# Five unread GpSimd multiplies behind every three indirect DMAs, pinned in program order

## The chip, the cores and the metric

The kernel runs on one core of one Trainium2 chip. The metric is the device time of one execution, in microseconds (us). The core's engines are named as the profile names them: PE (TensorE, the matrix multiplies; PEld its weight loads), DVE (VectorE), ACT (ScalarE), POOL (GpSimd) and SP (SyncE, which issues most of the DMAs). Each engine works through its own instructions in order; semaphores hold an instruction until what it needs is done.

## The reference

Attention in which a query sees only the keys of its own cluster, and behind it a feed-forward network (FFN) with three hidden products of which the largest is kept.

```python
batch, n_heads, seq, head_dim = (4, 8, 768, 64)      # 16 clusters per head
q_assign = argmax(q_n @ c_n)                          # nearest centroid of each query
k_assign = argmax(k_n @ c_n)                          # and of each key
mask = q_assign[:, :, :, None] == k_assign[:, :, None, :]
scores = where(mask, scale * q @ k.T, -1e9)
attn_out = softmax(scores) @ v
x = attn_out.transpose(0, 2, 1, 3).reshape(3072, 512)
h = maximum(maximum(x @ w1, x @ w2), x @ w3)          # 512 -> 768
out = h @ w_out                                       # 768 -> 512
```

## The kernel before, in words

The kernel doesn't compute all 768 x 768 scores. It sorts the tokens of each head by cluster into 1024 places (8 blocks of 128), so that only 8 blocks of 128 x 128 scores are needed. The sorting of keys and values, and the way back of the outputs, are done by indirect DMAs that POOL issues. A (batch, head) is called a head below; there are 32, in 4 batches of 8.

For each head, in this order:

- `split_kv` (L554 on ACT, L555 on DVE) scales keys and values and splits them into a high and a low half-precision part, `kv`.
- `scatter` (L578, POOL): 6 indirect DMAs, one for each tile of 128 tokens, write rows of `kv` to their places in a buffer in device memory. Four such buffers are used in turn (`ring`, `kv_0` to `kv_3`). A scatter has a bounds check, for which POOL's sequencer sets a register just ahead of each DMA.
- `read_back` (L602 and the lines after it, SP) brings the sorted keys and values back as `kt` and `vt`.
- `order_q` (L622 on DVE builds one-hot rows `hot`; L624 on PE) sorts the queries by matrix multiply.
- `scores` (PE, DVE L660, ACT L665, DVE L670) and `values` (L684 to L686 on PE, L689 on DVE) make the outputs `of` of the sorted places, which SP writes to one of four buffers in device memory (`o_0` to `o_3`).
- `gather` (L699, POOL): 6 indirect DMAs fetch the rows of the head back in token order into `xb`, one tile of 128 tokens each. `xb` holds a whole batch, and there is one of it.

When the 8 heads of a batch are gathered, `x_split` (L273 on ACT, L274 on DVE, transposed by SP at L730) prepares the FFN's input; the FFN runs as L741 (hidden layers, PE, with DVE L753 and L758) and L774 (output, PE, with ACT L783). The FFN of batches 0 to 2 is spread over the heads of the next batch. The FFN of batch 3 can only come at the end.

The order of the work is set by a priority that a plan gives to each unit; a scheduler then lists each engine's instructions by these priorities and by when it takes their inputs to be ready. For head `k` of 32, the plan puts `scatter` at `k - 2.5` and `gather` at `k + 1.6`:

```python
put(max(k + h - 2, 0), when(k + h - 2.5, k), u["scatter"][h])
put(min(k + 1 + LATE, B * H), when(k + 0.6 + LATE, k), gather, b, h)
```

At the start POOL builds small tables for about 25 us; among these is `side` (128 x 4), made at L142, which eight multiplies `s_x * side` at L150 read.

Of the kernel before, what the change touches and what calls it, by code (L numbers as in the profile page):

```python
# [8 lines left out]
F32 = mybir.dt.float32  # L9
# [6 lines left out]
ALU = mybir.AluOpType  # L16
# [7 lines left out]
def sorted_attn__then__maxout_ffn(  # L24
# [17 lines left out]
    nc = tc.nc  # L42
# [3 lines left out]
    P = 128  # L46
# [27 lines left out]

    def const(shape, dt, name):
        return cpool.tile(shape, dt, name=name)

    def after(x, o, why=mybir.DependencyReason.DATA):
        tc.add_manual_dep(
            x.ins, o.ins.name, mybir.DependencyInfo(mybir.DependencyClass.Sync, why), reason="one of several places"  # L80
        )


    ident = const([P, P], F32, "ident")
    make_identity(nc, ident)
    ident16 = const([P, P], BF16, "ident16")
    nc.gpsimd.tensor_copy(ident16, ident)
    identh = const([P, P], F16, "identh")
    nc.gpsimd.tensor_copy(identh, ident)
    cw = const([P, H, 2 * C], F32, "cw")  # L90
# [51 lines left out]
    side = const([P, 4], F32, "side")  # L142
# [356 lines left out]
    def pair_units(b, pr):  # L499
# [67 lines left out]
        def index(h, n, u):  # L567
            a = 2 * (2 * (pr & 1) + h) + u
            return fours[b, pr // 2]["idx"][:, n, a : a + 1]
# [3 lines left out]
        def scatter(h):  # L573
            def f():
                at = (2 * g + h) % NRING
                sent = d["sent", h] = []
                for n in range(QT):
                    i = nc.gpsimd.indirect_dma_start(  # L578
                        out=ring[at],
                        out_offset=bass.IndirectOffsetOnAxis(ap=index(h, n, 1), axis=0),  # L580
                        in_=d["kv", h][:, n].rearrange("p a d -> p (a d)"),
                        in_offset=None,
                        bounds_check=NPLACE - 1,
                        oob_is_err=False,
                    )
                    for o in sent:
                        tc.declare_no_dep(i.ins, o.ins, reason="each place is one token's")
                    for o in ring_last[at]:
                        after(i, o, mybir.DependencyReason.ANTI)
                    sent.append(i)  # L590
                ring_last[at] = []

            return f
# [99 lines left out]
    def gather(b, h):  # L693
        d, i = st[b, h // 2], h & 1
        od = oring[(b * H + h) % NOUT]
        if b not in xb:
            xb[b] = sb.tile([P, QT, DM], F32, tag="xb", name="xb", bufs=NXB)
        for n in range(QT):
            nc.gpsimd.indirect_dma_start(  # L699
                out=xb[b][:, n, h * D : h * D + D],  # L700
                out_offset=None,
                in_=od,
                in_offset=bass.IndirectOffsetOnAxis(ap=d["index"](i, n, 0), axis=0),
            )

    x16, xsc = {}, {}

# [125 lines left out]
    for b in range(B):  # L833
        for h in range(H):
            k = b * H + h
            put(k, when(k, k), scores, b, h)
            put(k + 1, when(k + 0.5, k), values, b, h)
            put(min(k + 1 + LATE, B * H), when(k + 0.6 + LATE, k), gather, b, h)
        k = b * H + H + LATE
        if b + 1 < B:  # L840
            put(k + 1, k - 0.5, x_scale, b)
            for n in range(QT):
                put(k + 1, k - 0.5 + 0.01 * n, x_split, b, n)
            units = [u for gi in range(NG) for u in ffn_units(b, gi)]
            spread(units, k + 1, k + H + 1 + (F2 if b == 2 else 0), 0)
# [778 lines left out]
```

## Time and profile before

| | |
|---|---|
| median of 3 runs | 772.13 us (768.11 to 774.67) |
| profiled execution | 773.91 us, of which 772.2 us are the span of the profile |
| mean granted clock of PE | 0.885 of full speed |
| busy share of the span | PE 80%, DVE 61%, POOL 55%, ACT 53% |
| POOL's indirect DMAs | 384: 192 scatters and 192 gathers |

A row of a group of instructions gives the line, engine and operation, the tiles written and read, how often it ran, its busy time and the mean duration of one in ns, and then how long the engine stood idle just ahead of these instructions and what ended that idle time. An idle time put down to "issue" is one in which the engine waited for nothing that the profile shows.

### The profile page before, as it was taken

How to read it: one execution, taken by the hardware profiler on the slowest of the kernel's cores; microseconds unless marked ns; L12 is line 12 of the kernel's file. 1: busy time of each engine (PE TensorE's matmuls, PEld its weight loads, DVE VectorE, ACT ScalarE, POOL GpSimd, SP SyncE). 2: the span in 40 equal slices, each digit the busy share in tenths (PEclk: the TensorE clock that was granted, in tenths of full speed). 3: DMA queues.
4: the chain of work that ended last, by engine and by line, in shares of the span. 5: the costliest groups of instructions: out<-in, count | busy, mean ns of one | idle time of the engine just before them, and what ended most of it. 6: DMA issues, size and time to landing. Idle time of an engine off the chain costs nothing.

```text
span 772.2 us, 12828 instructions
## 1 busy us (share of the span) xinstructions
PE 621.5 (80%) x4284; PEld 352.6 (46%) x4313; DVE 473.8 (61%) x1202; ACT 410.9 (53%) x978; POOL 426.4 (55%) x478
## 2 busy tenths in 40 slices
PE   3466446566527899999999998988799999999993
PEld 1233223334314465555455655644366465564651
DVE  4787867887588888586769765775554324121220
ACT  2567665977585666564867655565644413211111
POOL 6374577777765467777767575767276544000000
PEclk8579756557658899999999999999899999999998
DMA  9778879999699567898976656477845434200001
GB/s 319 272 214 188 224 179 221 271 220 255 180 265 184 138 144 204 172 217 172 215 172 162 130 135 176 118 154 138 163 90 113 120 77 84 69 1 28 14 1 46
DMA packets 231197, 120.54 MB, mean 156 GB/s; under 512 B 200656, under 2 KB 209872, under 8 KB 231120
## 3 DMA queue, kind: packets, MB, share of 16 engines
q1 hardware_dynamic: 218832, 100.72, 55.1%
q0 software_dynamic: 12288, 18.90, 9.7%
q8 instruction: 36, 0.59, 0.3%
q14 instruction: 41, 0.34, 0.1%
HBM read 58.75 MB, written 29.36 MB: 114 GB/s over the span
## 4 chain that ended last, share of the span: by engine, by line
PE 42%; DMA 15%; issue 13%; POOL 12%; DVE 9%; ACT 6%; SPq 2%; POOLq 0%; DVEq 0%; ACTq 0%
PE one L741 24%; PE one L774 9%; POOL kv L578 6%; POOL xb L699 5%; PE big L624 4%; DMA kv<-kv,cl_idx 4%; DMA xb<-o,cl_idx 3%; ACT e L665 2%; DMA o<-of 2%; DMA x<-xh 2%; DVE hot L622 2%; DMA wd<-in_moe_w_dram 1%; DVE kv L555 1%; DMA kt<-kv 1%; PE big L656 1%
## 5 line engine op out<-in xcount | busy, mean ns | idle before, releaser
L741 PE MATMUL one<-x,w 128*128 128x384 f16 x1728 | 296.6, 329 | 12.4 <-DVE wf_h L753 4.0
L699 POOL DMA_INDIRECT xb<-o,cl_idx x192 | 195.5, 1018 | 132.8 <-DMA o<-of 70.5
L578 POOL DMA_INDIRECT kv<-kv,cl_idx x192 | 212.5, 1107 | 85.0 <-issue 51.5
L741 PEld LDWEIGHTS <-w 128*128 128x128 f16 x1728 | 168.8, 99 | 126.7 <-issue 20.1
L624 PE MATMUL big<-hot,q 128*128 128x512 f16 x384 | 122.9, 442 | 47.9 <-DVE q L565 19.8
L665 ACT ACTIVATE e<-big,nm,sc_al 128x128 f32<-128x128 f32 x256 | 113.6, 462 | 29.2 <-DVE nm L661 16.2
L622 DVE TENSOR_SCALAR hot<-line,cl_code 128x1024 f16<-128x1024 f16 x192 | 92.3, 498 | 5.5 <-PE big L624 5.1
L624 PEld LDWEIGHTS <-q 128*128 128x128 f16 x384 | 37.6, 107 | 92.7 <-issue 46.9
L753 DVE SCALAR_TENSOR_TENSOR wf_h<-one,wf_h 128x384 f32<-128x384 f32 x48 | 26.6, 554 | 55.4 <-PE one L741 55.3
L753 DVE SCALAR_TENSOR_TENSOR vf_h<-one,vf_h 128x384 f32<-128x384 f32 x48 | 26.7, 555 | 51.0 <-PE one L741 51.0
L665 ACT ACTIVATION_READ_ACCUMULATOR e<-big,nm,sc_al 128x1 f32 x256 | 53.4, 209 | 0.0
L774 PE MATMUL one<-wo,wf_h 128*128 128x512 f16 x216 | 49.3, 386 | 1.5 <-ACT o L783 0.8
L774 PE MATMUL one<-wo,vf_h 128*128 128x512 f16 x216 | 48.7, 379 | 1.4 <-ACT o L783 1.4
L660 DVE TENSOR_REDUCE nm<-big 128x8 f32<-128x1024 f32 x32 | 39.0, 1217 | 16.0 <-PE big L658 8.6
L684 PE MATMUL one<-vt,pt 128*128 128x64 f16 x256 | 29.5, 203 | 21.3 <-DMA pt<-hl 18.9
L632 ACT CAST qt<-big 128x1024 f16<-128x1024 f32 x32 | 32.5, 1014 | 22.0 <-PE big L624 17.0
L783 ACT ACTIVATE o<-one,so 128x512 f32<-128x512 f32 x24 | 15.9, 685 | 51.4 <-PE one L774 40.0
L515 ACT ACTIVATE junk<-rows 128x768 bf16<-128x768 f32 x32 | 27.0, 843 | 30.1 <-DVE cl_code L467 20.0
L670 DVE SCALAR_TENSOR_TENSOR hl<-e,hl 128x1024 f16<-128x1024 f32 x32 | 38.9, 1214 | 5.4 <-ACT hl L669 5.3
L554 ACT ACTIVATE kv<-rows,sc_s 128x384 f16<-128x384 f32 x64 | 35.8, 613 | 8.7 <-DVE sc_s L542 8.7
L689 DVE TENSOR_TENSOR of<-one,r 128x512 f32<-128x512 f32 x32 | 21.9, 685 | 29.6 <-PE one L686 27.5
L555 DVE SCALAR_TENSOR_TENSOR kv<-rows,sc_s,kv 128x384 f16<-128x384 f32 x64 | 37.5, 611 | 2.8 <-ACT kv L554 2.7
(212 smaller groups left out, 890.3 us busy)
## 6 DMA issues: line engine op xcount, KB each, us to landing
stage<-in_qk_dram SPq DMA_DIRECT2D x32, 384.0 KB
wd<-in_moe_w_dram SPq DMA_DIRECT2D x18, 512.0 KB
vt<-kv SPq DMA_DIRECT2D x32, 256.0 KB
o<-of SPq DMA_DIRECT2D x32, 256.0 KB
rows<-in_kr_dram SPq DMA_DIRECT2D x16, 384.0 KB
rows<-in_v_dram SPq DMA_DIRECT2D x16, 384.0 KB
rows<-in_qr_dram SPq DMA_DIRECT2D x16, 384.0 KB
out_dram<-o SPq DMA_DIRECT2D x24, 256.0 KB
```

The costliest lines, as they stand in the source:

```text
L554: nc.scalar.activation(kv[:, :, at], x, AF.Copy, scale=s[:, i : i + 1])
L555: nc.vector.scalar_tensor_tensor(kv[:, :, at + 1], x, s[:, i : i + 1], kv[:, :, at], op0=ALU.mult, op1=ALU.subtract)
L578: i = nc.gpsimd.indirect_dma_start(out=ring[at], out_offset=bass.IndirectOffsetOnAxis(ap=index(h, n, 1), axis=0), in_=d["kv", h][:, n].rea ...
L622: nc.vector.tensor_scalar(a, line, code, None, op0=ALU.is_equal)
L624: nc.tensor.matmul(t[:, lo : lo + 512], d["q16"][:, h * QT + n].rearrange("p a d -> p (a d)"), a[:, lo : lo + 512], start=(n == 0), stop=( ...
L660: nc.vector.tensor_reduce(nm, ts, axis=AX.X, op=ALU.max)
L665: nc.scalar.activation(x[:, j], ts[:, j], AF.Exp, bias=nm[:, j : j + 1], scale=d["al"], accum_out=sm[:, j : j + 1])
L670: nc.vector.scalar_tensor_tensor(hl[:, 1], x, 2.0**14, hl[:, 0], op0=ALU.mult, op1=ALU.subtract)
L699: nc.gpsimd.indirect_dma_start(out=xb[b][:, n, h * D : h * D + D], out_offset=None, in_=od, in_offset=bass.IndirectOffsetOnAxis(ap=d["inde ...
L741: nc.tensor.matmul(t[:, 0:NB], w16[:, jt, wa, i, ct], x16[b, gi][:, :, xa * CT + ct, :], start=(n == 0), stop=(n == 3 * CT - 1),)
L753: nc.vector.scalar_tensor_tensor(m, t[:, 0:NB], 2.0**-23, ms[jt], op0=ALU.mult, op1=ALU.max)
L774: nc.tensor.matmul(t[:, 0:DM], h16[jt][:, ha, tt * P : (tt + 1) * P], wo16[:, jt, wa, :], start=(n == 0), stop=(n == 3 * JT - 1),)
```

## The change

A 128 x 4 tile `blank` is added. `scatter` and `gather` call a new function `spaced` behind each of their 6 indirect DMAs (n = 0 to 5). It pins the DMA, except for n = 0, behind the instruction that was written last on POOL, and behind n = 2 and n = 5 it adds five multiplies `blank = side * side` on POOL, each pinned in the same way. Nothing reads `blank`.

```diff
+    blank = const([P, 4], F32, "blank")
+
+    def spaced(i, n):
+
+        if n:
+            tc.keep_in_program_order(i)
+        for _ in range(5 if n % 3 == 2 else 0):
+            tc.keep_in_program_order(nc.gpsimd.tensor_tensor(blank, side, side, op=ALU.mult))
...
                     for o in ring_last[at]:
                         after(i, o, mybir.DependencyReason.ANTI)
+                    spaced(i, n)
                     sent.append(i)
...
-            nc.gpsimd.indirect_dma_start(
+            got = nc.gpsimd.indirect_dma_start(
                 out=xb[b][:, n, h * D : h * D + D],
...
+            spaced(got, n)
```

A pin is an order of issue on one engine and no wait. But all the multiplies write the same tile, so each one also waits on a semaphore until the one before it is done; they form one chain in the order in which they are written. In all there are 32 heads x 2 x 2 x 5 = 640 of them. The line of the scatter becomes L587, that of the gather L709, and the multiplies stand at L85.

On POOL, where the scatters and gathers begin, the order before was this (`kv16` is the head's `kv` tile, and a row that ends in x6 is six instructions in a row):

```order
L578 DMA kv_0_226<-kv16_394,cl_idx_352 1024x256 x6
L578 DMA kv_1_227<-kv16_414,cl_idx_352 1024x256 x6
L578 DMA kv_2_228<-kv16_459,cl_idx_352 1024x256 x6
L578 DMA kv_3_229<-kv16_544,cl_idx_352 1024x256 x6
L699 DMA xb_952<-o_0_231,cl_idx_352 128x64 x6
```

At the same place the changed kernel has this:

```order
L587 DMA kv_0_227<-kv16_395,cl_idx_353 1024x256 x3
L85 TENSOR_TENSOR blank_72<-side_119 128x4
L587 DMA kv_0_227<-kv16_395,cl_idx_353 1024x256 x3
L587 DMA kv_1_228<-kv16_415,cl_idx_353 1024x256 x6
L85 TENSOR_TENSOR blank_72<-side_119 128x4 x4
L587 DMA kv_2_229<-kv16_470,cl_idx_353 1024x256
L85 TENSOR_TENSOR blank_72<-side_119 128x4
L587 DMA kv_2_229<-kv16_470,cl_idx_353 1024x256 x5
L85 TENSOR_TENSOR blank_72<-side_119 128x4
L587 DMA kv_3_230<-kv16_565,cl_idx_353 1024x256 x6
L85 TENSOR_TENSOR blank_72<-side_119 128x4 x33
L709 DMA xb_1003<-o_0_232,cl_idx_353 128x64 x3
```

The scatters aren't parted by five multiplies: the instruction written last ahead of a scatter is the setting of its register, so its pin holds it behind that and not behind the multiplies, and these are put off and stand in bunches, here 33 ahead of the first gather. The gathers have no such register and are parted as written.

At the end of the heads, the last rows of POOL before were these gathers, of heads 26 to 31 if the first is 0:

```order
L699 DMA xb_6692<-o_2_233,cl_idx_5094 128x64 x6
L699 DMA xb_6692<-o_3_234,cl_idx_5094 128x64 x6
L699 DMA xb_6692<-o_0_231,cl_idx_6106 128x64 x6
L699 DMA xb_6692<-o_1_232,cl_idx_6106 128x64 x6
L699 DMA xb_6692<-o_2_233,cl_idx_6106 128x64 x6
L699 DMA xb_6692<-o_3_234,cl_idx_6106 128x64 x6
```

In the changed kernel the last twelve rows are these, halves of the gathers of heads 28 to 31:

```order
L709 DMA xb_7223<-o_0_232,cl_idx_6587 128x64 x3
L85 TENSOR_TENSOR blank_72<-side_119 128x4 x10
L709 DMA xb_7223<-o_1_233,cl_idx_6587 128x64 x3
L85 TENSOR_TENSOR blank_72<-side_119 128x4
L709 DMA xb_7223<-o_2_234,cl_idx_6587 128x64 x3
L85 TENSOR_TENSOR blank_72<-side_119 128x4 x9
L709 DMA xb_7223<-o_2_234,cl_idx_6587 128x64 x3
L85 TENSOR_TENSOR blank_72<-side_119 128x4
L709 DMA xb_7223<-o_3_235,cl_idx_6587 128x64 x3
L85 TENSOR_TENSOR blank_72<-side_119 128x4 x9
L709 DMA xb_7223<-o_3_235,cl_idx_6587 128x64 x3
L85 TENSOR_TENSOR blank_72<-side_119 128x4 x5
```

Each head's gather has become two halves with multiplies between and ahead of them. Over the whole program the 640 multiplies stand in 93 bunches, of 1 to 33. The scheduler has also moved instructions of the other engines against each other; from the last values on, PE and DVE have the same order as before.

## The prediction

> **What bounds the kernel now.** I read the rows of busy time by slice first, then the busy time by stage, then POOL's groups and waits, and the chain at the end.
>
> ```profile
> PE   3466446566527899999999998988799999999993
> POOL 6374577777765467777767575767276544000000
> ```
>
> PE is full only from about a third of the span on. POOL looks half busy throughout and has nothing to do in the last sixth. By stage, from the first scatter to the last gather and beyond:
>
> ```profile
> core 0: us, PE busy (x) PEld busy (x) DVE busy (x) ACT busy (x) POOL busy (x), PEclk, DMA share, GB/s
> 100.00:200.00 100.00, 60.18 (x408) 32.83 (x411) 78.52 (x207) 74.75 (x173) 77.97 (x72) 0.64 0.95 228
> 250.00:400.00 150.00, 142.41 (x1095) 83.14 (x1103) 117.54 (x312) 95.73 (x236) 102.04 (x98) 0.98 0.83 183
> 400.00:550.00 150.00, 133.97 (x972) 78.12 (x979) 100.63 (x236) 88.43 (x225) 99.54 (x93) 0.97 0.63 143
> 651.00:772.00 121.00, 107.88 (x608) 59.27 (x606) 24.88 (x45) 21.24 (x39) 0.00 (x0) 0.97 0.11 30
> ```
>
> From 100 to 200 us POOL's 72 DMAs take 78 us; from 250 to 550 us PE is busy for 276 of 300 us. But busy time understates POOL, as its own timeline shows (start, duration, and in brackets the idle time ahead):
>
> ```profile
> 113.02 1.09 POOL L699 DMA_INDIRECT xb<-o,cl_idx  x1 [0.30 <-issue]
> 114.41 0.94 POOL L699 DMA_INDIRECT xb<-o,cl_idx  x1 [0.30 <-issue]
> 115.66 1.14 POOL L699 DMA_INDIRECT xb<-o,cl_idx  x1 [0.30 <-issue]
> ```
>
> Between two indirect DMAs POOL loses 0.30 us in which nothing is waited for. So 72 of them fill 78 + 72 x 0.30 = 99.6 of the 100 us: in that stage POOL is full. The groups and their real waits for the whole run:
>
> ```profile
> L578 POOL DMA_INDIRECT kv<-kv,cl_idx x192 | 212.5, 1107 | 85.0 <-issue 51.5 <-DVE kv L555 28.0 <-DMA xb<-o,cl_idx 0.9
> L699 POOL DMA_INDIRECT xb<-o,cl_idx x192 | 195.5, 1018 | 132.8 <-DMA o<-of 70.5 <-issue 53.3 <-DVE xh L274 5.6
> POOL xb L699 <- DMA o<-of: 70.5, 14, 14.0
> POOL kv L578 <- DVE kv L555: 28.0, 5, 12.1
> POOL xb L699 <- DVE xh L274: 5.6, 1, 5.6
> POOL xb L699 <- DVE worow L322: 2.7, 1, 2.7
> ```
>
> The idle time adds up to 85.0 + 132.8 = 217.8 us. The four waits make 70.5 + 28.0 + 5.6 + 2.7 = 106.8; the other 111.0 are the 0.30 gaps. The tables ahead of the first scatter and the last gather have these rows:
>
> ```profile
> 22.27 2.79 POOL L170 TENSOR_SCALAR k_line<-k_line,block 128x128 f16<-128x128 f16 x8
> 649.51 1.30 POOL L699 DMA_INDIRECT xb<-o,cl_idx  x1 [0.30 <-issue]
> span 772.2 us, 12828 instructions
> ```
>
> So POOL's path is closed: 25.06 us of tables (22.27 + 2.79), 408.0 us in DMAs, 111.0 us in gaps and 106.8 us of waiting give 650.9 us, which is where the last gather ends (649.51 + 1.30 = 650.8). **POOL is bound for 544 of its first 651 us, and only 107 us of slack lie in them.** Behind that comes a tail in which POOL has no part:
>
> ```profile
> 653.93 11.81 PE one L774 x54
> 665.75 35.10 PE one L741 x216
> 713.49 35.10 PE one L741 x216
> ```
>
> From the end of the last gather to the end of the span it is 772.2 - 650.8 = 121.4 us: the FFN of batch 3, and ahead of it the L774 block of batch 2, whose last DVE step is queued behind the split of the last gathered tiles.
>
> **The change part by part.** It removes nothing. It adds 640 multiplies to POOL, and it moves DMAs.
>
> *One multiply.* The trace has eight of the same shape and operation, at L150:
>
> ```profile
> L150 POOL TENSOR_TENSOR s_x<-s_x,side 128x4 f32<-128x4 f32 x8 | 1.6, 198 | 0.3
> 17.26 0.20 POOL L150 TENSOR_TENSOR s_x<-s_x,side 128x4 f32<-128x4 f32 x1
> 17.39 0.13 POOL L149 MEMSET s_x<- 128x1 f32 x2
> 17.60 0.20 POOL L150 TENSOR_TENSOR s_x<-s_x,side 128x4 f32<-128x4 f32 x1
> ```
>
> It takes 0.198 us. The instruction behind one at 17.26 needs nothing of it and starts 0.13 us later, so an unchained multiply costs POOL 0.13 us. The multiply at 17.60 needs the memsets that end at 17.39 + 0.13 = 17.52 and starts 0.08 us behind them. A chained one, which waits for its predecessor's end, should cost 0.198 + 0.08 = 0.28 us. The `blank` multiplies are all chained, so I take 0.28: **640 x 0.28 = 179 us** more on POOL's path. Ends: 640 x 0.13 = 83 us if the chain doesn't keep them from overlapping; for the upper end see the third rival.
>
> *The gap of 0.30 us.* The trace doesn't show whether it stands ahead of an indirect DMA or behind it, since nothing else ever stands between two. If a bunch fills a gap, 93 bunches save up to 93 x 0.30 = 28 us; if a gap stands on both sides of a bunch, they cost 28 us more. I take none, which lies between.
>
> *What the 179 us meet.* The slack is 106.8 us. Two parts of it can be placed: the first wait, 10.75 of the 28.0 us on L555, stands ahead of the first scatter, with no multiply ahead of it, and stays. The longest, 14.0 us ahead of the first gather, has a bunch of 33 in front (33 x 0.28 = 9.2 us) and shrinks to 5. The other 82 us are some 18 waits for outputs (`o<-of`) or split keys, most of them after 220 us. As the DMAs slow down, each head has more time to become ready, so most of these go; a bunch that stands behind a wait doesn't hide in it, though, and in-order queues on SP and DVE can hold a head up for a late gather. I keep a quarter, 20 us, which makes 36 us of waiting left. Ends: none of the rest, 16; or all of it, 107.
>
> *What is queued behind the waits.* Behind each multiply that waits stand gathers and scatters. A late scatter holds SP's read of `kt`, then the scores on PE; a late gather holds DVE's split of `xb` and, through the four `o` buffers, SP's next write of `o`. So POOL's delay reaches every engine, and PE's FFN work no longer covers it, since a pace of POOL's is slower than PE's: PE's 499 busy us (its row below) stay under the new path.
>
> ```profile
> 36.00:651.00 615.00, 498.91 (x3605) 287.51 (x3635) 428.07 (x1085) 374.67 (x914) 407.83 (x384) 0.88 0.75 173
> ```
>
> *The moved DMAs.* Halved gathers come later by at most their bunches, which are counted already. The tail behind the last gather keeps its order on PE and DVE, and its 121.4 us; the last gather again comes last on POOL, with only 5 multiplies behind it.
>
> *The sum.* 25 + 408 + 111 + 179 + 36 = 759 us to the last gather, + 121.4 = 880 us of span, + 1.7 us that the profiled execution (773.91) has beside its span (772.2) = 882. The median of the runs lies 1.8 us below the profiled execution, so **880 us**, 108 us or 14% slower.
>
> **The rivals.**
>
> *Cheap multiplies.* They overlap, at 0.13 us each, or fill the gaps. For it: the 0.13 above. Against it: each waits for its predecessor. With 83 us, of which some 50 fall into the slack, the last gather comes at 25 + 519 + 83 + 57 = 684 and the time is 684 + 121 + 2 = 807; with 0.28 and filled gaps, 852.
>
> *Faster.* The one mechanism that I see: halving the gathers and moving scatters ahead of the second halves takes the 14 waits on `o<-of` away, 70.5 us, while the multiplies cost less than that. It decides below 70.5 / 640 = 0.11 us for one multiply; the lowest row gives 0.13. PE would then bound it: from 250 to 550 us it has only 24 us idle, so at best about 750.
>
> *Dearer multiplies.* Indirect DMAs get longer beside DVE work:
>
> ```profile
> 35.43 1.01 DVE L565 SCALAR_TENSOR_TENSOR q<-rows,sc_s,q 128x768 f16<-128x768 f32 x1
> 35.81 1.75 POOL L578 DMA_INDIRECT kv<-kv,cl_idx  x1 [10.75 <-DVE kv L555]
> 37.23 1.14 DVE L555 SCALAR_TENSOR_TENSOR kv<-rows,sc_s,kv 128x384 f16<-128x384 f32 x2
> 37.86 2.01 POOL L578 DMA_INDIRECT kv<-kv,cl_idx  x1 [0.30 <-issue]
> 43.23 0.97 POOL L578 DMA_INDIRECT kv<-kv,cl_idx  x1 [0.30 <-issue]
> L578 POOL DMA_INDIRECT kv<-kv,cl_idx x192: 966/981/2363, 35.8 to 583.4; - x192
> ```
>
> They take 1.75 and 2.01 us there and 0.97 where DVE does small things. Over all 192 scatters the mean, 1.107, lies 0.13 above the median, 0.981. If each multiply lost the same 0.13, it would cost 0.41 and all of them 262 us: 25 + 519 + 262 + 36 = 842, and 965 us in the end. The same time comes out, 953, if all 107 us of waits stay beside 179. Against it: DVE is busy for 428 of 615 us, but a multiply of 0.2 us offers less to hit than a DMA of 1 us.
>
> The Trainium skill, page "SBUF — State Buffer", section "Who interferes with whom", names this: a DVE instruction with two inputs in SBUF blocks a GpSimd instruction that reads SBUF for its whole length, and the other way round. The slow pair beside L565 and L555, which have two such inputs, agrees; whether a short multiply that reads `side` suffers as much, no row shows. By that rule the time would go toward this rival's.
>
> *No change.* The scatters aren't spaced as the code reads, but the 640 multiplies are all issued. Staying within 1% needs all 179 us hidden in 107 us of slack, or multiplies that run under the DMAs. I give it little.
>
> **How the numbers follow.** My forecast (840 to 920): 0.60. Cheap multiplies (800 to 840): 0.17. Dearer multiplies or unshrunk waits (920 to 970): 0.16. No change: 0.04. Faster: 0.03. The range reaches to the cheap end, 807, and most of the way to the dear one: 805 to 950. A measurement of this kernel tells about 1% from no change; by the cases: faster by over 1% 0.03, within 1% 0.04, slower by over 1% 0.93.
>
> **What would show it.** In the profile of the changed kernel: 640 multiplies at L85 of about 0.2 us busy, 0.28 us apart inside a bunch; indirect DMAs as before, near 1.0 to 1.1 us; POOL's waits on `o<-of` far below 70.5 us; the last gather near 760 us and a tail of about 121 us. Wrong would be: multiplies 0.13 or 0.4 us apart, the first DMA behind a bunch without its 0.30 us (or more of it), waits that stay above 90 us, or a tail that grows because PE's clock or a queue changed there.

## The result and the profile after

The changed kernel takes **882.01 us** (median of 4 runs, 879.1 to 883.53) against 770.92 us (4 runs, 768.11 to 774.67) for the kernel before on the same chip: a ratio of 1.143, with a 95% interval of 1.137 to 1.149. Where the runs of a kernel fall into a faster and a slower group, a ratio in this document is one of the faster runs alone. Its profiled execution took 879.1 us, of which 877.4 us are the span of the profile.

From the page of the changed kernel, the span, the busy rows by slice, and the chain that ended last by engine and by line:

```profile
span 877.4 us, 13478 instructions
PE   3554565534456998795697796956889995599995
POOL 7477878878787787787877777777777777500000
POOL 38%; issue 17%; PE 16%; DMA 13%; DVE 8%; ACT 5%; SPq 1%; POOLq 0%; DVEq 0%; ACTq 0%
```

The chain of the kernel before had this row:

```profile
PE 42%; DMA 15%; issue 13%; POOL 12%; DVE 9%; ACT 6%; SPq 2%; POOLq 0%; DVEq 0%; ACTq 0%
```

The run of nines that PE had in the middle of the span is gone, while POOL stands at 7 to 8 tenths until the last gather. The chain now passes through POOL for 38% of the span instead of 12%, and 17% more are "issue", most of it on POOL, ahead of its DMAs and between its multiplies.

POOL's groups of the changed kernel (busy time, mean of one in ns, idle time ahead and what ended it), from the list of groups:

```profile
L587 POOL DMA_INDIRECT kv<-kv,cl_idx x192 | 207.1, 1078 | 68.9 <-issue 51.1 <-DVE kv L564 10.8 <-DVE r L684 0.7
L709 POOL DMA_INDIRECT xb<-o,cl_idx x192 | 191.9, 999 | 52.6 <-issue 44.8 <-DMA o<-of 2.6 <-DVE nm L670 0.3
L85 POOL TENSOR_TENSOR blank<-side 128x4 f32<-128x4 f32 x640 | 172.7, 270 | 44.3
```

The waits on `o<-of` fell from 70.5 us to 2.6, and those on `kv` from 28.0 to 10.8; the latter is one wait, ahead of the first scatter. The multiplies, which wait for nothing but each other, cost 172.7 + 44.3 = 217.0 us. By stage, as before (the span, then the busy time of PE, PEld, DVE, ACT and POOL, then PE's granted clock, the DMA share and GB/s):

```profile
100.00:200.00 100.00, 51.57 (x386) 28.04 (x390) 71.96 (x189) 64.67 (x146) 79.86 (x121) 0.69 0.85 212
250.00:400.00 150.00, 124.86 (x925) 74.21 (x930) 104.69 (x273) 85.42 (x220) 118.60 (x221) 0.90 0.67 147
400.00:550.00 150.00, 111.01 (x782) 63.22 (x789) 79.28 (x192) 67.25 (x169) 117.92 (x223) 0.90 0.55 127
757.00:877.00 120.00, 110.06 (x613) 60.29 (x611) 24.87 (x45) 21.14 (x39) 3.51 (x8) 0.97 0.11 31
```

From 250 to 550 us PE was busy for 276 of 300 us before, and for 236 now: its work is stretched over a longer time, as the chain through POOL also says. The last 120 us look as they did.

On POOL's own timeline (start, duration, idle time ahead in brackets) the steps of the prediction can be read one by one; these are five places of the changed kernel:

```profile
39.12 1.48 POOL L587 DMA_INDIRECT kv<-kv,cl_idx  x1 [0.30 <-issue]
40.62 0.22 POOL L85 TENSOR_TENSOR blank<-side 128x4 f32<-128x4 f32 x1
40.99 1.01 POOL L587 DMA_INDIRECT kv<-kv,cl_idx  x1 [0.16 <-issue]
42.31 0.97 POOL L587 DMA_INDIRECT kv<-kv,cl_idx  x1 [0.30 <-issue]
...
52.35 1.06 POOL L85 TENSOR_TENSOR blank<-side 128x4 f32<-128x4 f32 x4
54.03 1.38 POOL L587 DMA_INDIRECT kv<-kv,cl_idx  x1 [0.61 <-DVE s_at L456]
...
69.85 12.74 POOL L85 TENSOR_TENSOR blank<-side 128x4 f32<-128x4 f32 x33
83.63 0.99 POOL L709 DMA_INDIRECT xb<-o,cl_idx  x1 [1.03 <-DMA o<-of]
...
107.30 0.94 POOL L709 DMA_INDIRECT xb<-o,cl_idx  x1 [0.30 <-issue]
108.26 4.32 POOL L85 TENSOR_TENSOR blank<-side 128x4 f32<-128x4 f32 x9
...
759.11 0.94 POOL L709 DMA_INDIRECT xb<-o,cl_idx  x1 [0.31 <-issue]
760.07 1.38 POOL L85 TENSOR_TENSOR blank<-side 128x4 f32<-128x4 f32 x5
```

Five multiplies behind the last gather take 1.38 us, 0.276 each, which is the predicted 0.28. Nine at 108.26 take 0.48 each, and 33 at 69.85 take 0.386 each. What DVE does beside the nine is on its timeline:

```profile
108.05 1.14 DVE L564 SCALAR_TENSOR_TENSOR kv<-rows,sc_s,kv 128x384 f16<-128x384 f32 x2
109.11 0.48 DVE L632 TENSOR_SCALAR hot<-line,cl_code 128x1024 f16<-128x1024 f16 x1
109.50 1.01 DVE L574 SCALAR_TENSOR_TENSOR q<-rows,sc_s,q 128x768 f16<-128x768 f32 x1
110.43 1.14 DVE L564 SCALAR_TENSOR_TENSOR kv<-rows,sc_s,kv 128x384 f16<-128x384 f32 x2
```

Apart from `hot` (L632), which has one tensor as input, these are the instructions with two inputs in SBUF beside which the prediction found slow indirect DMAs. That the DMAs were slow for the same reason is not shown.

### The profile page after: what moved, and what is told of

Read it like the earlier page. It is cut to its first block, busy times and chain, and to the rows that moved or that the text cites. A ratio compares the mean times of both kernels' runs of the same rounds, so it can differ in the third digit from the quotient of the medians.

```text
span 877.4 us, 13478 instructions
## 1 busy us (share of the span) xinstructions
PE 630.4 (72%) x4284; PEld 355.6 (41%) x4313; DVE 479.7 (55%) x1202; ACT 410.3 (47%) x978; POOL 589.9 (67%) x1118
## 4 chain that ended last, share of the span: by engine, by line
POOL 38%; issue 17%; PE 16%; DMA 13%; DVE 8%; ACT 5%; SPq 1%; POOLq 0%; DVEq 0%; ACTq 0%
POOL xb L709 15%; POOL blank L85 12%; PE one L752 10%; POOL kv L587 10%; PE one L785 4%; DMA xb<-o,cl_idx 3%; ACT e L675 2%; DMA kv<-kv,cl_idx 2%; DMA pt<-hl 2%; DMA o<-of 2%; DMA wd<-in_moe_w_dram 2%; DMA rows<-in_qr_dram 1%; DVE hot L632 1%; DVE kv L564 1%; DMA rows<-in_v_dram 1%
## 5 line engine op out<-in xcount | busy, mean ns | idle before, releaser
L752 PE MATMUL one<-x,w 128*128 128x384 f16 x1728 | 304.7, 335 | 43.4 <-DVE wf_h L764 18.4
L587 POOL DMA_INDIRECT kv<-kv,cl_idx x192 | 207.1, 1078 | 68.9 <-issue 51.1
L752 PEld LDWEIGHTS <-w 128*128 128x128 f16 x1728 | 171.6, 100 | 162.2 <-issue 59.1
L709 POOL DMA_INDIRECT xb<-o,cl_idx x192 | 191.9, 999 | 52.6 <-issue 44.8
L85 POOL TENSOR_TENSOR blank<-side 128x4 f32<-128x4 f32 x640 | 172.7, 270 | 44.3
L634 PE MATMUL big<-hot,q 128*128 128x512 f16 x384 | 122.1, 435 | 52.6 <-DVE hot L632 26.4
L632 DVE TENSOR_SCALAR hot<-line,cl_code 128x1024 f16<-128x1024 f16 x192 | 93.8, 503 | 41.2 <-PE big L634 40.5
L634 PEld LDWEIGHTS <-q 128*128 128x128 f16 x384 | 37.5, 106 | 97.3 <-issue 52.6
L764 DVE SCALAR_TENSOR_TENSOR wf_h<-one,wf_h 128x384 f32<-128x384 f32 x48 | 26.6, 555 | 62.0 <-PE one L752 59.8
L283 DVE SCALAR_TENSOR_TENSOR xh<-xb,xsc,xh 128x512 f16<-128x512 f32 x24 | 18.0, 749 | 76.7 <-ACT xh L282 76.7
L282 ACT ACTIVATE xh<-xb,xsc 128x512 f16<-128x512 f32 x24 | 17.3, 720 | 86.4 <-DMA xb<-o,cl_idx 75.5
L764 DVE SCALAR_TENSOR_TENSOR vf_h<-one,vf_h 128x384 f32<-128x384 f32 x48 | 26.5, 552 | 46.0 <-PE one L752 38.2
L666 PE MATMUL big<-kt,qt 128*128 128x128 f16 x256 | 26.6, 252 | 34.7 <-DMA kt<-kv 32.6
```

The lines of the kernel that those rows point to most:

```text
L85: tc.keep_in_program_order(nc.gpsimd.tensor_tensor(blank, side, side, op=ALU.mult))
L587: i = nc.gpsimd.indirect_dma_start(out=ring[at], out_offset=bass.IndirectOffsetOnAxis(ap=index(h, n, 1), axis=0), in_=d["kv", h][:, n].rea ...
L632: nc.vector.tensor_scalar(a, line, code, None, op0=ALU.is_equal)
L634: nc.tensor.matmul(t[:, lo : lo + 512], d["q16"][:, h * QT + n].rearrange("p a d -> p (a d)"), a[:, lo : lo + 512], start=(n == 0), stop=( ...
L709: got = nc.gpsimd.indirect_dma_start(out=xb[b][:, n, h * D : h * D + D], out_offset=None, in_=od, in_offset=bass.IndirectOffsetOnAxis(ap=d ...
L752: nc.tensor.matmul(t[:, 0:NB], w16[:, jt, wa, i, ct], x16[b, gi][:, :, xa * CT + ct, :], start=(n == 0), stop=(n == 3 * CT - 1),)
```

## The experiments

The theory: POOL's path sets the time, and the whole 14% comes from the 640 steps standing on it: their own duration, their chain, and a stretch beside DVE. The rivals: the pins or the halved gathers do it; the number of steps matters and not what they cost; the stretch comes with a step's length and not with its reading of SBUF.

The variants below change only what the diff shows. Since the scheduler also orders by when it takes things to be ready, some instructions of the other engines change places as well, so a difference of a few us between two variants isn't put down to their steps.

### A first round on a chip that was slower itself

Four variants ran on a chip on which the kernel before took 936.7 us (921.95 to 944.73, 7 runs) instead of 771. Their edits are those of `e9_ten`, `e6_two`, `e7_unchained` and `e8_memset` below.

> Ten multiplies instead of five behind every third indirect DMA, 1280 in all. Theory (POOL's path sets the pace, and its slack is used up): each further multiply costs what the 640 cost, 217.0 us / 640 = 0.34 us, so 640 x 0.34 = 217 us on top of 882, about 1100 us, with the last gather near 980 us and the tail still 117 to 121 us. If the multiplies get shorter because DVE is spread thinner (0.31 each), about 1060. Rival (the order of the halved gathers costs the time, not the multiplies themselves): about 880, as with five.

> Two multiplies instead of five, 256 in all. Theory: POOL has 256 x 0.34 = 87 us more to do and had 107 us of waits to hide it in, of which 11 us can't be used; the loss is far below the proportional one: 775 to 805 us, with waits of 40 to 80 us left on POOL. Rival 1 (loss in proportion to the number, no slack): 771 + 111 x 256 / 640 = 815 us. Rival 2 (the order of the halved gathers costs the time): about 880.

> The same 640 multiplies with the same pins, but each writes one of four columns (128 x 1) in turn, so that it needs only the one four before it and can start before its predecessor ends. Theory: a multiply costs 0.13 us unchained instead of 0.28, plus what DVE adds (0.06): 640 x 0.19 = 122 us on POOL, with some 25 us of waits left, about 797 us. Rival (the chain costs nothing, POOL's own step costs 0.34): 882.

> The same 640 steps, chained and pinned as before, but each is a memset of the tile, which reads nothing. Theory: 0.10 us for the memset (the 128 x 1 ones took 0.098) + 0.08 for the chain = 0.18 us, 115 us in all, 25 us of waits left, about 790 us if a step that only writes isn't held up by DVE. Rival 1 (it is held up as much as the multiplies, 0.06 us each): 0.24 x 640 = 154 us, about 825. Rival 2 (order of the halved gathers): about 880.

Measured: ten steps 1068.09 us (ratio 1.151, 1.120 to 1.183), two steps 915.82 (0.988, 0.973 to 1.004), the unchained steps 902.23 (0.971, 0.934 to 1.008) and the memsets 913.93. Three of the four lie far above what was expected and ten steps below its 1100 us, but these times can't be held against numbers that were worked out from a kernel of 771 us. By their intervals, two steps and the unchained steps don't even differ from the kernel before as measured there. The chain of the variant with two steps shows stretches like these:

```profile
527.87 17.78 another core or an unknown queue
578.75 20.45 another core or an unknown queue
```

The chains of all four variants on that chip have such stretches, the longest of each 10 to 20 us; the chains of the profiles from the other chips have none over 3 us. What held the kernel there stays open. The four were run again elsewhere, where the kernel before took 770.7 us (768.11 to 772.88, 7 runs).

### No pins

```diff
-        if n:
-            tc.keep_in_program_order(i)
...
-            tc.keep_in_program_order(nc.gpsimd.tensor_tensor(blank, side, side, op=ALU.mult))
+            nc.gpsimd.tensor_tensor(blank, side, side, op=ALU.mult)
```

> The same 640 chained multiplies, without any pin: 45 of them float ahead of the first scatter, each gather stays whole, the other 595 stand in 70 bunches among the DMAs. Theory (POOL pays for each multiply, wherever it stands): 595 x 0.34 = 202 us on POOL's path, up to 45 x 0.28 = 13 us more hidden in the first wait; the last gather some 10 us earlier than with the pins, 865 to 885 us where the kernel before takes 771, a ratio of 1.12 to 1.15. Rival (the pins, which halve the gathers and hold them back, cost a good part of it): 800 to 840 us, 1.04 to 1.09.

878.69 us, ratio 1.137 (1.131 to 1.142), as with pins; the kernel before took 772.08 us there (7 runs). 45 of the multiplies have floated ahead of the first scatter, and the other 595 stand in 70 bunches. In the trace the gathers are nearly whole, not wholly so: in 15 of the 32 groups of six no multiply stands between the DMAs, in the other 17 a single one does. Its groups on POOL:

```profile
L709 POOL DMA_INDIRECT xb<-o,cl_idx x192 | 195.2, 1017 | 58.9 <-issue 56.5 <-DMA o<-of 1.4 <-DVE worow L333 0.5
L85 POOL TENSOR_TENSOR blank<-side 128x4 f32<-128x4 f32 x640 | 172.5, 270 | 44.9
```

So without pins, and with no bunch inside a gather, the time stays within 1%; the rival's 800 to 840 us is out. And it isn't the halving that takes the waits on `o<-of` away: they go to 1.4 us without it, because POOL now comes to a gather later than its outputs do. Pins without multiplies were not run.

### Fewer and more steps

Two steps for five:

```diff
-        for _ in range(5 if n % 3 == 2 else 0):
+        for _ in range(2 if n % 3 == 2 else 0):
```

> Two multiplies instead of five, 256 in all, on a chip on which the kernel before takes about 771 us. Theory: POOL has 256 x 0.34 = 87 us more to do and 107 us of waits to hide it in, of which 11 us can't be used; the loss is well below the proportional one: 775 to 805 us, with 40 to 80 us of waits left on POOL. Rival 1 (in proportion to the number, no slack): 771 + 111 x 256 / 640 = 815 us. Rival 2 (the halving of the gathers costs the time): about 880.

809.45 us, ratio 1.050 (1.046 to 1.053): 4 us over the range, nearer to the rival's 815. The groups and the waits that are left:

```profile
L709 POOL DMA_INDIRECT xb<-o,cl_idx x192 | 196.6, 1024 | 96.3 <-issue 45.2 <-DMA o<-of 38.9 <-DVE w_s L335 6.6
L85 POOL TENSOR_TENSOR blank<-side 128x4 f32<-128x4 f32 x256 | 81.4, 318 | 14.6
```

256 steps put 96.0 us on the path, 0.375 each, and 38.7 us of them came through. The real waits left on POOL are 60.2 us (38.9 on `o<-of`, 13.6 on `kv`, 6.6 and 1.1 others), inside the expected 40 to 80. So slack isn't used up before the time begins to grow: a wait takes in only a bunch that stands ahead of it, and a bunch in a place without a wait goes straight into the time.

Ten steps for five (`range(10 if ...`):

> 1280 multiplies. The run on the other chip gave 418 us for them on POOL (323.8 busy + 94.4 idle, 0.327 us each). Theory: 24 + 394 + 108 + 418 + 13 of waits, last gather at 957, time 957 + 117 + 2 = 1076 us, 1060 to 1095: nothing of the second 640 is hidden any more. Rival (other work hides part of them): below 1040.

1044.88 us, ratio 1.356 (1.351 to 1.361). The last gather ends at 956.6 us, as expected (957); the time was expected at 1060 to 1095 and is lower. What differs is the tail, which is 1042.7 - 956.6 = 86 us instead of 117. On PE's timeline:

```profile
932.01 5.42 PE L752 MATMUL one<-x,w 128*128 128x384 f16 x24 [33.86 <-DMA x<-xh]
938.01 17.71 PE L752 MATMUL one<-x,w 128*128 128x384 f16 x108 [0.58 <-ACT vf_h L762]
958.09 15.49 PE L752 MATMUL one<-x,w 128*128 128x384 f16 x84 [2.37 <-ACT vf_h L762]
986.00 35.26 PE L752 MATMUL one<-x,w 128*128 128x384 f16 x216
```

132 of the 216 matmuls of a hidden block (24 + 108) run here before the last gather has ended; only 84 and the second block come behind it. The output block of batch 2 (54 matmuls, 11.82 us), which stood in the tail of the changed kernel, also runs earlier here, at 886.33. The order at the end is another one: by POOL's timeline 9 gathers and 60 multiplies stand behind the first half of the last head's gather, where the changed kernel has 3 gathers and 9 multiplies, so the first three tiles of `xb` can be split, and multiplied, that much ahead of the end. The time lies between the two ranges: the theory is right for POOL's path, and the rival (other work hides part of the steps, below 1040 us) for the tail.

### What a step does

Two variants of 640 steps on that chip, and two more on a chip with the kernel before at 772.21 us (768.16 to 773.98, 7 runs). Unchained: a multiply of one column, which takes the next of four columns each time.

```diff
-    blank = const([P, 4], F32, "blank")
+    blank, turn = const([P, 4], F32, "blank"), [0]
...
-            tc.keep_in_program_order(nc.gpsimd.tensor_tensor(blank, side, side, op=ALU.mult))
+            turn.append(c := (turn[-1] + 1) % 4)
+            x = side[:, c : c + 1]
+            tc.keep_in_program_order(nc.gpsimd.tensor_tensor(blank[:, c : c + 1], x, x, op=ALU.mult))
```

> 640 multiplies with the same pins, each into one of four columns (128 x 1) in turn, so that each needs only the one four before it. The run on the other chip gave 137.9 us for them on POOL (136.4 busy + 1.5 idle, 0.215 us each) instead of 217.0. Theory (POOL's path sets the pace): 24 + 399 + 108 + 138 + about 25 of waits puts the last gather at 694 and the time at 694 + 117 + 2 = 813 us, 795 to 825. Rival (POOL's time isn't what counts, the number of steps or their places are): about 880.

833.9 us, ratio 1.082 (1.078 to 1.085), 9 us over the range. The steps cost what was expected (140.2 us against 138). What was taken too low are the waits left on POOL (27.8 + 11.1 + 2.0 = 40.9 us, not 25) and the DMAs (206.6 + 201.6 = 408.2 us, not 399). A memset, which only writes:

```diff
-            tc.keep_in_program_order(nc.gpsimd.tensor_tensor(blank, side, side, op=ALU.mult))
+            tc.keep_in_program_order(nc.gpsimd.memset(blank, 0.0))
```

> 640 memsets instead of multiplies, chained and pinned as in the changed kernel. They read nothing. The run on the other chip gave 105.9 us for them on POOL (73.7 busy + 32.2 idle, 0.165 us each). Theory: 24 + 399 + 108 + 106 + 35 of waits, last gather at 672, time 672 + 117 + 2 = 791 us, 775 to 805, and below the unchained multiplies. Rival (a step costs the same whatever it does, or the order counts): about 880.

802.38 us, ratio 1.040 (1.036 to 1.044), inside the range, near its upper end. But a memset is also half as long as a multiply, so a stretch in proportion to length could be small for that reason. A counter (`iota`) also only writes, and was made longer:

```diff
-    blank = const([P, 4], F32, "blank")
+    blank = const([P, 32], F16, "blank")
...
-            tc.keep_in_program_order(nc.gpsimd.tensor_tensor(blank, side, side, op=ALU.mult))
+            tc.keep_in_program_order(nc.gpsimd.iota(blank, pattern=[[1, 32]], base=0, channel_multiplier=0, ...))
```

> 640 counters of 128x32 f16 in place of the multiplies: they write SBUF and read nothing, and by the rows of the counters ahead of the first scatter (129 ns at 128x8, 984 ns at 128x1024) should take about 150 ns alone, between the memset's 101 and the multiply's 198. If only a step that reads SBUF is stretched beside DVE, the mean lies 15 to 30 ns above the median, as with the memsets (+18), a step costs 0.22 us with its chain, POOL's path gains 140 us and the time is 825 to 845. If any step is stretched in proportion to its length, as the multiplies by 72/198, the mean lies 55 ns above the median, a step costs 0.26 us, POOL's path gains 165 us and the time is 845 to 865.

830.49 us, ratio 1.076 (1.071 to 1.081), in the range for a stretch that comes with reading. And a copy, which reads one operand (`nc.gpsimd.tensor_copy(blank, side)` in the multiply's place):

> 640 copies of side into blank (128x4 f32) in place of the multiplies: one operand is read from SBUF where a multiply reads two. A copy of 128x1 takes 188 ns in the early rows. If any read of SBUF meets DVE's blocking, the mean lies 60 to 75 ns above the median as with the multiplies, and the time is within 1% of theirs, 870 to 890. If it takes two operands to be hit, the mean lies 15 to 35 ns above the median, a step costs 0.28 instead of 0.34 us and the time is 835 to 860.

882.9 us, ratio 1.144 (1.139 to 1.149), the same as with the multiplies. In part that is chance: the copies cost POOL 17 us less than the multiplies, but about 14 us more of waits are left (13.5 of them for DVE's split of `xb`) and the DMAs take 6.5 us more. The groups of the four variants, in the order above:

```profile
L87 POOL TENSOR_TENSOR blank<-side 128x1 f32<-128x1 f32 x640 | 138.6, 254 | 1.6
```

```profile
L85 POOL MEMSET blank<- 128x4 f32 x640 | 75.9, 119 | 31.4
```

```profile
L85 POOL IOTA blank<- 128x32 f16 x640 | 112.5, 176 | 38.1
```

```profile
L85 POOL COPY blank<-side 128x4 f32<-128x4 f32 x640 | 166.6, 260 | 33.7
```

And one step of the same lines in ns, shortest, median and longest (first the changed kernel, then the same four):

```profile
L85 POOL TENSOR_TENSOR blank<-side x640: 197/198/2052, 40.6 to 761.3; 128x4 f32<-128x4 f32 x160
```

```profile
L87 POOL TENSOR_TENSOR blank<-side x640: 184/186/1552, 40.8 to 713.9; 128x1 f32<-128x1 f32 x160
```

```profile
L85 POOL MEMSET blank<- x640: 101/101/708, 41.3 to 683.3; 128x4 f32 x160
```

```profile
L85 POOL IOTA blank<- x640: 157/158/537, 40.4 to 712.0; 128x32 f16 x160
```

```profile
L85 POOL COPY blank<-side x640: 183/188/1263, 40.7 to 765.3; 128x4 f32<-128x4 f32 x160
```

The mean less the median is the stretch. The three steps that read SBUF have 72, 68 and 72 ns; the two that only write have 18 and 18, though a counter of 158 ns is nearer to the readers in length than to the memset. In proportion to length the counter would have had 57 (158 x 72/198). One operand read is enough.

Beside which instructions of DVE the stretch arises can be counted in the traces. Each step is put to the DVE instruction that it overlaps longest, and its stretch is its duration less the median of all 640. The cells give the number of steps and their mean stretch in ns:

| beside on DVE | multiplies | copies | counters | memsets |
|---|---|---|---|---|
| SCALAR_TENSOR_TENSOR, two inputs in SBUF (L564, L574, L680, L283 and others) | 88: 410 | 105: 343 | 129: 3 | 183: 2 |
| SCALAR_TENSOR_TENSOR, one of two inputs in PSUM (L764) | 49: 2 | 40: 1 | 40: 2 | 41: 2 |
| TENSOR_SCALAR `hot` (L632), one input | 56: 109 | 44: 137 | 50: 161 | 48: 188 |
| no DVE instruction | 243: 2 | 265: 2 | 230: 3 | 189: 3 |

Three places show it, a multiply and six memsets beside `hl` (two inputs in SBUF) and one memset beside `hot`:

```profile
74.39 1.23 DVE L680 SCALAR_TENSOR_TENSOR hl<-e,hl 128x1024 f16<-128x1024 f32 x1
74.43 1.25 POOL L85 TENSOR_TENSOR blank<-side 128x4 f32<-128x4 f32 x1
...
351.12 1.22 DVE L680 SCALAR_TENSOR_TENSOR hl<-e,hl 128x1024 f16<-128x1024 f32 x1
351.23 0.89 POOL L85 MEMSET blank<- 128x4 f32 x6
...
457.97 0.48 DVE L632 TENSOR_SCALAR hot<-line,cl_code 128x1024 f16<-128x1024 f16 x1
458.02 0.46 POOL L85 MEMSET blank<- 128x4 f32 x1
```

So there are two effects. A DVE instruction with two SBUF inputs holds up a step that reads SBUF, and not one that only writes; it makes 36.1 of the multiplies' 46.0 us of stretch. This is what the Trainium skill says on its page "SBUF — State Buffer", section "Who interferes with whom": a DVE instruction with two SBUF inputs contends with a GpSimd instruction that reads SBUF, and not with one that only writes. The traces agree, with 410 ns for the multiplies and 343 for the copies against 3 and 2 for the writers. The other effect is `hot`, which has one input and holds up all four kinds; it makes 6.1 of the multiplies' 46.0 us, and 9.0 of the 11.2 us that the memsets are stretched by. No variant takes these DVE instructions away; the counts are from traces in which they stand beside the steps by chance.

The runs on the chips where the kernel before took 771 to 772 us, side by side. A step's cost is its busy time and the idle time ahead of it; the last gather's end and the tail behind it are from the same profile:

| steps | us each | on POOL, us | `o<-of` waits, us | last gather ends | tail | time, us |
|---|---|---|---|---|---|---|
| none (before) | | 0 | 70.5 | 650.8 | 121.4 | 771 |
| 256 multiplies | 0.375 | 96.0 | 38.9 | 688.1 | 122.0 | 809.5 |
| 640 memsets | 0.168 | 107.3 | 21.0 | 682.7 | 119.7 | 802.4 |
| 640 unchained | 0.219 | 140.2 | 27.8 | 713.3 | 120.6 | 833.9 |
| 640 counters | 0.235 | 150.6 | 10.2 | 711.1 | 118.5 | 830.5 |
| 640 copies | 0.313 | 200.3 | 3.2 | 764.3 | 121.5 | 882.9 |
| 640 multiplies | 0.339 | 217.0 | 2.6 | 760.1 | 117.3 | 882.0 |
| 640, no pins (45 ahead of the first scatter) | 0.340 | 217.4 | 1.4 | 753.7 | 122.7 | 878.7 |
| 1280 multiplies | 0.323 | 413.7 | 8.2 | 956.6 | 86.1 | 1044.9 |

640 instructions cost between 32 and 111 us, so it isn't their number. From none to 640 multiplies, 217 us of steps put the last gather 109 us later; from 640 to 1280 it is 196.5 us for 196.7. So once the waits are gone, POOL's time counts in full. Between neighbours in the table the order isn't strict: the copies come 4 us behind the multiplies with 17 us less on POOL, and the counters 2 us ahead of the unchained steps with 10 us more, since the waits left over differ by as much.

## Why the prediction was right, and where its terms were off

The forecast case came in: 880 us predicted, 882.0 measured. The mechanism was right in its main steps, but the sum was right in part by luck, because errors of nearly the same size stood against each other.

- **POOL's path sets the end.** Shown: last gather at 760.05 us (759.11 + 0.94) against 759, and over the variants it moves from 683 us with the memsets to 957 with 1280 multiplies.
- **The tail stays.** 117.3 us against 121.4. It stays at 117 to 123 us in all variants but the one with ten steps, where the order at the end changed. That the order there stays was the prediction's premise.
- **One multiply at 0.28 us: too low by a fifth.** Alone it is right (0.276). The mean is 217.0 / 640 = 0.339, which makes 217 us instead of 179, 38 more. The missing part is the stretch beside DVE. It was priced in the rival of dearer multiplies at 0.13 us for one step, and this was too much, 0.072 by the mean less the median. The forecast left it at nothing, since a multiply of 0.2 us offers less to hit than a DMA; for its length it is hit harder, 0.072 of 0.198 us against the scatters' 0.13 of 0.98. The chain was right: 44.3 / 640 = 0.07 us of idle time ahead of one, against 0.08, and 1.6 us in all where the steps aren't chained.
- **Waits of 36 us left: too many.** 10.8 + 2.6 = 13.4 us are left, 23 fewer. The prediction kept a quarter of the movable waits for heads that late gathers would hold up; there are hardly any here. The first wait (10.75 us then, 10.8 now) stayed as said, and the one ahead of the first gather shrank from 14.0 to 1.03 us rather than to 5, since its bunch of 33 took 12.74 us instead of 9.2.
- **The DMAs and gaps.** 207.1 + 191.9 = 399.0 us against 408, 9 less: the scatters' mean went from 1107 to 1078 ns and the gathers' from 1018 to 999. The gaps come to 68.9 + 52.6 - 13.4 = 108.1 us against 111; see the last section. Of the signs that the prediction named for being wrong, this one came: the first DMA behind a bunch doesn't have its 0.30 us. It is worth a few us. Another came in places, multiplies 0.4 us apart and more (0.48 in the bunch at 108.26), but not in the mean.

So the terms were 38 too low and 23 + 9 + 3 + 4 = 39 too high (waits, DMAs, gaps, tail). Tables and reading errors of a few us aside, that is the whole of it. The profiled execution took 879.1 us against 882 in the sum; that the median came so near to 880 also rests on the profiled run being the shortest of the four this time. By the prediction's own wait term, the right price of a multiply would have given 918 us. Of the rivals, cheap multiplies fall by 0.339 us; the memsets, at 0.168, come near to that case, 802.4 us against the 807 that was worked out for it at 0.13. "Faster" falls with it: its point of decision was 0.11 us, and even the memset is above that. "No change" falls by the time. "Dearer multiplies" was the right mechanism at half its price.

## What to carry to other kernels

An engine that is idle for a third of the time up to its last instruction can still set the time: add its gaps and its real waits to its busy time before calling it free, and look for slack in the waits. Steps put on such an engine are free only where a wait stands behind them; here the waits, 107 us before and 13 after, took 93 of the first 217 us and nothing of the next 197. For filling time on GpSimd beside a busy VectorE, a step that only writes is the cheap one here: price anything that reads SBUF by its mean in a busy stage, not by its duration in a quiet one.

## What the runs showed of the hardware that was not expected

- **The gap of 0.30 us stands ahead of an indirect DMA, and about half of it can be covered.** In the timeline of the changed kernel a multiply starts right behind the DMA's end (40.62 against 39.12 + 1.48 = 40.60), and the DMA behind the multiply starts 0.16 us behind that (the bracket at 40.99) instead of 0.30. The prediction took no gain from it. Of the 92 DMAs that stand behind multiplies, 75 have 0.14 to 0.16 us ahead of them; but 14 have 0.43 to 0.71, like the one at 54.03, for which no cause was found, one has 0.29 and two wait for `o<-of`. The 75 save about 11 us and the 14 give back about 4. The gaps in all are only 3 us less than before, because DMAs that waited before now show a gap of their own.
- **DVE's durations don't grow.** POOL's steps are stretched, up to 2.05 us for one multiply of 0.198. The other direction, of which the prediction speaks, isn't seen: DVE's instruction with two SBUF inputs keeps its mean beside 640 multiplies, the kernel before first. Whether such an instruction starts later for a multiply was not looked at.

```profile
L555 DVE SCALAR_TENSOR_TENSOR kv<-rows,sc_s,kv 128x384 f16<-128x384 f32 x64 | 37.5, 611 | 2.8 <-ACT kv L554 2.7
L564 DVE SCALAR_TENSOR_TENSOR kv<-rows,sc_s,kv 128x384 f16<-128x384 f32 x64 | 37.6, 610 | 1.6 <-ACT kv L563 0.9 <-DMA wd<-in_moe_w_dram 0.5
```

- **One chip was 21% slower for the same kernel**, 936.7 us against 771. PE's granted clock was 0.83 to 0.84 there against 0.88 to 0.91 on the two others; whether that is cause or consequence isn't shown, and no cause was found.
